# Masking keys from an SBUF copy on VectorE, epsilon inside the normalisation statistics, and a new instruction order, in a four-block attention kernel

## The chip, the cores and the metric

The kernel runs on one core of one Trainium2 chip. The metric is the time of one execution on the device, in microseconds (us). A core has TensorE (PE in the profile, with PEld for its weight loads), VectorE (DVE), ScalarE (ACT), GpSimd (POOL) and SyncE (SP), each with its own queue of instructions that runs in order; engines wait for each other through semaphores. SP, ACT and POOL also issue DMA transfers. SBUF is the working memory, PSUM the eight banks that TensorE writes its results to.

## The reference

The input x is 2048 tokens of 512 numbers in bfloat16. Four blocks follow each other, each with a normalisation in front and a residual behind: linear attention (A), attention in a sliding window of 256 tokens (B), and the same two again with the same weights.

```python
def _layernorm(x, axis=-1, eps=1e-5):
    m = jnp.mean(x, axis=axis, keepdims=True)
    v = jnp.var(x, axis=axis, keepdims=True)
    return (x - m) / jnp.sqrt(v + eps)

# A: 32 heads of 16
phi = lambda t: jnp.where(t > 0, t + 1, jnp.exp(t)) + 1e-6
pq, pk = phi(q), phi(k)
kv = jnp.einsum("bhsd,bhse->bhde", pk, v)
z = jnp.einsum("bhsd->bhd", pk)
o = jnp.einsum("bhqd,bhde->bhqe", pq, kv) / (jnp.einsum("bhqd,bhd->bhq", pq, z)[..., None] + 1e-6)

# B: 32 heads of 16, W = 256
scores = jnp.einsum("bhqd,bhkd->bhqk", q, k) * (Dh ** -0.5)
mask = (idx[:, None] - idx[None, :] >= 0) & (idx[:, None] - idx[None, :] < W)
o = jnp.einsum("bhqk,bhkd->bhqd", _softmax(jnp.where(mask, scores, -1e9)), v)

x = x + _A_ref(_layernorm(x), A_wqkv, A_wo)
x = x + _B_ref(_layernorm(x), B_wqkv, B_wo)
x = x + _A_ref(_layernorm(x), A_wqkv, A_wo)
x = x + _B_ref(_layernorm(x), B_wqkv, B_wo)
```

## The kernel before

The tokens are cut into 16 tiles of 128, which stay in SBUF (`xres`) from start to end. The work has three passes. Pass 1 (operations named `1.`) normalises each tile and sums the keys and values of the first A block. Pass 2 finishes that block tile by tile (`2.`), does the first B block (`2.b.` for queries, keys and values, `2.a.` for the attention) and, as tiles become final, sums the keys and values of the second A block (`2k.`). Pass 3 finishes the second A block (`3.`) and does the second B block (`3.b.`, `3.a.`). Pass 2 can't begin its A outputs before pass 1 has summed all tiles, nor pass 3 before `2k.` has.

**Normalisation** (`ln`, lines 808 to 821). For each of 64 tiles VectorE takes statistics of the 512 numbers (`.st`, line 813), which are two triples, one for every second number; aggregates them into mean and variance (`.ag`, line 814); and adds epsilon to the variance (`.ae`, line 816). GpSimd raises that to the power -1/2 (`.rs`, line 817), and VectorE subtracts and multiplies (`.xn`, line 819). The result is transposed, by a DMA that SP issues (line 827), or for a few tiles (`BYPE`) by TensorE with a copy out of PSUM (lines 834 and 844).

**Keys of a B tile** (`b_qkv`, lines 960 to 983). TensorE computes the projected keys into one PSUM bank (`k0`, `k1`, eight small multiplies each, line 869). The key matrix that the scores use, `kbd`, holds each block of 64 keys twice, once with every second group of 16 rows set to zero and once with the others, so that one multiply of 32 rows serves two heads. Two operations `kb0` and `kb1` write these two forms, both from PSUM, each multiplying by a column of zeros and ones (`mab`), on ScalarE or VectorE as the order says (line 970). Queries and values are copied out of PSUM once each (`qc`, `vc`, line 844), and GpSimd issues four DMAs for each tile that spread the values (`vbd`, line 980).

**Attention of a B tile** (`b_attn`, lines 985 to 1139). TensorE computes scores for the window in five steps into pairs of PSUM banks (lines 1006 and 1055), ScalarE takes exponentials of 128x1024 (lines 1034 and 1076), VectorE masks the ends of the window (lines 1042 and 1094), TensorE multiplies by the values (lines 1112 and 1124), VectorE divides (lines 1134 and 1136), and the output projection and residual follow (lines 857 and 893). The last tile of pass 3 goes through `b_end`, cut finer.

**Order.** Nothing is ordered at run time. `ORDER` (lines 328 to 430) is a list of operation numbers written out in advance: the position in it gives each engine's sequence, an apostrophe takes the second of two possible engines, and what follows a colon names the buffers taken. `schedule` walks through the list, and `emit` sets the waits that the data need. The costs written in the operations (0.595 and so on) take part only in the choice of buffers where the list names none. Operations are numbered as the code creates them, so one that is added or left out shifts all the later numbers. The operations called `jump` stand for a branch in each engine's queue, and where they stand in the list is where the engine branches.

**Loads.** SP issues the tiles of x and most weights (`load`, line 774), and the same queue carries the DMA transposes. In the list before, SP issues x, then the twelve transposes of pass 1's tiles from tile 4 on, then four of the five weights that pass 2 needs, the fifth later.

Of the kernel before, what the change touches and what calls it, by code (L numbers as in the profile page):

```python
# [8 lines left out]
ACT = mybir.ActivationFunctionType  # L9
# [3 lines left out]
P = 128  # L13
D = 512
# [304 lines left out]
def _act_cost(n):  # L319
    return 0.055 + 0.000833 * n  # L320
# [29 lines left out]
933 476:3 477:3 939:1 672:5.1 673 962:6.0.2 961 686:4.0 963 964 700 487:2.3 488 701 674' 934 702:3 687 688 689 489 490 491:0 492:0 940:5 941 942 943:0  # L350
1019:0.6.2 1020 1021 501 944 690:3.2 691 987 478:2 954:0.4.0 955 956 692' 953 1022 479 678 1416:3.1 1417 716 993:0.6.4 1418' 911:5 912 965 994 995 480 913
1419 966:0.3.5 703:3 967 711:2.2.0 502:6.1 945:1 660 661 957 503 504 505 493:5 494 495 968 969 712 713 997:0.3.1 998 999 506:2 970:5 975:2 971 1054:0.6.0 717
718 719 734 735 972 976 977 1055 1056 752 753 989:0.3.0 679 990 973:2 974:3 978:3 979 1000 704:5.1 988 705 706' 707' 736 708:2.3 737 996 709 710' 714 991 992
1028:0.6.3 1029 1030 1420 1421 720:1 507:3 508:4 1422 693:5.1.1 694 695' 1001:0.2.2 1002 1003 509 510 946:7 947 948 1032:0.5.5 1033 1005:4 1006 1004 1423:2
980:2 1034 738:0 511:7.12.1 1010:3 1433 1434 1435 1007 721:2 1008:0 1009:0 1089:0.5.1 981:2 982 1090 1091 1058 1436 512 1424:0 696 697 515 513 1437:3 770
1411:4.1.0 1412 983 1447 1448 1449 1450 1024:0.5.0 1025 1026 1011 1012 1013:1 1014 1031 726:7.0 727 728' 1413 1414 1415 1063:0.2.4 722:6.2 723 1451:1 1027
# [15 lines left out]
1509:1 1510:9 818' 1234:0.6.0 1235 1538 1539:2 1220:2 1705:3.17.3 1241 1236 1237 1706 1221 1222 1223:0 1224 1709 786 1540:8 2716 1273:0.4.4 1274 1461:7.6 1462
# [995 lines left out]
```

## Time and profile before

| | |
|---|---|
| median of 3 runs | 419.46 us (419.31 to 419.74) |
| span of the profiled execution, first to last instruction | 417.1 us |
| granted TensorE clock | 1.000 |
| exponentials on ScalarE, 128x1024 from PSUM | 240 + 56, mean 1.10 us each |
| DMA, mean over the span | 71 GB/s |

Of the profiled execution only the span is recorded, not its time with what lies around it; the median is 2.4 us above the span. In the views that follow an engine's busy time counts the stretch in which at least one of its instructions was open, so two neighbours that overlap are not counted twice; the mean of one instruction is its whole duration, overlap included. A chain of waits is followed back from the last instruction, at each step to whatever released it. "Idle before" is the time for which an engine stood without work in front of an instruction, with the engine that ended it.

### The profile page before, as it was taken

To read this page: it belongs to the slowest core of one execution; us is meant where nothing else is said; L and a number is where in the kernel's file an instruction comes from. 1 tells how busy PE (TensorE), PEld (TensorE's weight loads), DVE (VectorE), ACT (ScalarE), POOL (GpSimd) and SP (SyncE) were. 2 spreads that over 40 slices of the span, in tenths; PEclk is the share of its full clock that TensorE was granted. 3 is DMA by queue.
4 is the path that set the end of the run, shared out by engine and by line. 5 is a ranking of instruction groups with operands and counts; after the bars stand their busy time and mean duration, and the time that the engine had idled before them with its cause. 6 is when DMAs were issued, how large, how long until landed. Compare 5 with 4: busy or idle time off the path is not lost.

```text
span 417.1 us, 18964 instructions
## 1 busy us (share of the span) xinstructions
PE 401.3 (96%) x8402; PEld 283.5 (68%) x8402; DVE 379.2 (91%) x998; ACT 383.3 (92%) x499; POOL 106.7 (26%) x202
## 2 busy tenths in 40 slices
PE   8999999999999999999999999889999999999997
PEld 3654776765767686776686677567676676677775
DVE  6999899999999999999898899999999998979784
ACT  4977979999999999999999677899999999999996
POOL 2331024521343022124150101161333113404100
DMA  8436435343243222324112201331445253243142
GB/s 273 135 63 166 113 53 123 75 55 61 54 77 51 40 48 48 41 53 85 35 40 57 43 2 39 65 81 32 81 66 82 50 72 63 55 85 54 38 93 79
DMA packets 76808, 29.48 MB, mean 71 GB/s; under 512 B 66352, under 2 KB 74672, under 8 KB 76720
## 3 DMA queue, kind: packets, MB, share of 16 engines
q1 hardware_dynamic: 71424, 22.63, 27.0%
q0 software_dynamic: 4096, 4.46, 5.8%
q8 instruction: 68, 1.11, 1.2%
q10 hardware_dynamic: 1200, 1.11, 0.8%
q14 instruction: 20, 0.16, 0.1%
HBM read 6.29 MB, written 2.10 MB: 20 GB/s over the span
## 4 chain that ended last, share of the span: by engine, by line
ACT 47%; PE 41%; DVE 10%; issue 1%; DVEq 0%
ACT pF L1076 33%; PE ps L857 17%; ACT pH L1034 9%; PE ps L869 8%; PE ps L1055 4%; PE ps L1124 4%; PE ps L1112 2%; PE ps L915 2%; ACT kbd L970 2%; DVE o L953 1%; DVE xres L892 1%; DVE stats L813 1%; ACT E L878 1%; PE ps L1253 1%; ACT vt L844 1%
## 5 line engine op out<-in xcount | busy, mean ns | idle before, releaser
L1076 ACT ACTIVATE pF<-ps 128x1024 bf16<-128x1024 f32 x240 | 231.0, 1095 | 2.7 <-PE ps L1055 2.0
L817 POOL TENSOR_TENSOR rstd<-mv,const 128x1 f32<-128x1 f32 x64 | 39.7, 622 | 208.9 <-DVE mv L816 200.1
L980 POOL DMA_DIRECT2D vbd<-vt x128 | 67.0, 532 | 81.1 <-DVE vt L844 61.6
L1034 ACT ACTIVATE pH<-ps 128x1024 bf16<-128x1024 f32 (+1 forms) x64 | 60.5, 1032 | 3.1 <-PE ps L1006 3.0
L1124 PE MATMUL ps<-vbd,pF 128*128 128x34 bf16 x1856 | 59.6, 178 | 0.0
L1124 PEld LDWEIGHTS ps<-vbd,pF 128*128 128x128 bf16 x1856 | 52.9, 96 | 3.3 <-issue 0.2
L1055 PE MATMUL ps<-qT,kbd 32*128 32x128 bf16 x1920 | 49.0, 216 | 4.4 <-ACT pF L1076 1.2
L1094 DVE TENSOR_TENSOR pF<-pF,const 128x512 bf16<-128x512 bf16 (+2 forms) x116 | 46.7, 414 | 4.8 <-ACT pF L1076 4.6
L878 ACT ACTIVATE E<-ps 128x512 bf16<-128x512 f32 x64 | 39.5, 635 | 8.4 <-PE ps L857 4.3
L813 DVE BATCH_NORM_STATS2 stats<-xres 128x6 f32<-128x512 bf16 x64 | 43.8, 687 | 1.9 <-DMA xres<-in_A_x_dram 1.1
L1055 PEld LDWEIGHTS ps<-qT,kbd 32*128 32x128 bf16 x1920 | 28.7, 92 | 22.8 <-ACT pF L1076 9.4
L1042 DVE TENSOR_TENSOR pH<-pH,const 128x1024 bf16<-128x1024 bf16 (+1 forms) x64 | 40.8, 650 | 0.0
L857 PE MATMUL ps<-w_Bv,xT 128*128 128x512 bf16 (+2 forms) x152 | 35.7, 346 | 0.3 <-ACT vt L844 0.2
L869 PE MATMUL ps<-xT,w_Bk 128*128 128x128 bf16 x512 | 35.3, 219 | 0.3
L869 PE MATMUL ps<-xT,w_Bq 128*128 128x128 bf16 x512 | 35.2, 219 | 0.1
L857 PE MATMUL ps<-w_Ao,oT 128*128 128x512 bf16 (+2 forms) x144 | 34.5, 356 | 0.7 <-ACT pF L1076 0.6
L1112 PEld LDWEIGHTS ps<-vbd,pH 128*128 128x128 bf16 x928 | 28.6, 96 | 8.8 <-issue 1.8
L857 PE MATMUL ps<-w_Ak,xTa 128*128 128x512 bf16 (+1 forms) x134 | 33.6, 369 | 0.6 <-ACT xTa L844 0.5
L869 PE MATMUL ps<-xTa,w_Aq 128*128 128x128 bf16 x512 | 33.9, 219 | 0.2
L1112 PE MATMUL ps<-vbd,pH 128*128 128x34 bf16 x928 | 32.9, 178 | 1.1 <-ACT pF L1076 0.3
L857 PE MATMUL ps<-w_Bo,oT 128*128 128x512 bf16 (+2 forms) x140 | 33.0, 355 | 0.7 <-ACT pF L1076 0.6
L857 PE MATMUL ps<-w_Av,xTa 128*128 128x512 bf16 (+2 forms) x133 | 33.6, 371 | 0.0
(95 smaller groups left out, 622.4 us busy)
## 6 DMA issues: line engine op xcount, KB each, us to landing
vbd<-vt POOLq DMA_DIRECT2D x128, 34.0 KB, 2.1
xres<-in_A_x_dram SPq DMA_DIRECT2D x16, 128.0 KB, 4.9
out_dram<-xres SPq DMA_DIRECT2D x15, 128.0 KB, 1.9
oT<-o SPq DMA_TRANSPOSE x60, 2.6
w_Ak<-in_A_wqkv_dram ACTq DMA_DIRECT2D x1, 512.0 KB, 4.8
w_Av<-in_A_wqkv_dram ACTq DMA_DIRECT2D x1, 512.0 KB, 5.8
w_Aq<-in_A_wqkv_dram SPq DMA_DIRECT2D x1, 512.0 KB, 6.2
w_Ao<-in_A_wo_dram SPq DMA_DIRECT2D x1, 512.0 KB, 4.0
```

The lines of the kernel that those rows point to most:

```text
L813: s.op(n + ".st", {"DVE": 0.595}, lambda e, en: e.bn_stats(a_st, x.h[:]), reads=[x], writes=[st])
L857: i = e.matmul(g.h[:, a:b], xT.h[:, kt, :], w.h[:, kt, a:b], start=(kt == 0), stop=(kt == 3), skip_group_check=True)
L869: i = e.matmul(g.h[:, f * P:(f + 1) * P], w.h[:, kt, f * P:(f + 1) * P], xT.h[:, kt, :], start=(f == 0 and kt == 0), stop=(kt == 3), skip_ ...
L878: s.op(n + ".e", {"ACT": _act_cost(512)}, lambda e, en: e.activation(E.h[:], g.h, ACT.Exp, bias=0.0), reads=[g], writes=[E])
L980: return [e.dma_start(vbd.h[64 * a:64 * a + 64, j, a], vt.h[64 * j:64 * j + 64, a]) for j in range(2)]
L1034: return e.activation(d, c, ACT.Exp, bias=0.0, scale=DH ** -0.5)
L1042: return e.tensor_tensor(v, v, tr, ALU.mult)
L1055: i = e.matmul(ss[r // 2].h[:, r % 2, k * P:k * P + P], kbds[fj[m] // 2].h[32 * r:32 * r + 32, f, fj[m] % 2, :], qT.h[32 * r:32 * r + 32, ...
L1076: s.op("e%d%d" % (u, g), {"ACT": _act_cost(1024)}, lambda e, en, S=ss[g], pb=pb, g=g: e.activation(pb.h[:, 2 * g:2 * g + 2, :], S.h, ACT.E ...
L1094: return e.tensor_tensor(v, v, tr, ALU.mult)
L1112: i = e.matmul(U.h[:, c:c + 34], pH.h[:, 4 * r + f, 64 * a:64 * a + P], vbds[j // 2].h[:, j % 2, :, 4 * f + r, :], start=first[0], stop=Tr ...
L1124: i = e.matmul(U.h[:, c:c + 34], pFs[at[f, m][0]].h[:, r, at[f, m][1] * P:at[f, m][1] * P + P], vbds[fj[m] // 2].h[:, fj[m] % 2, :, 4 * f ...
```

## The change

Four things change.

1. The B block's keys are copied once from PSUM to SBUF (`kc`, in a new ring `kt` of three buffers, on ScalarE or VectorE), and `kb0` and `kb1` then read that copy, on VectorE alone. One tile, tile 0 of pass 3 (`KNEAR`), keeps the old form.
2. The statistics of a tile get nine columns in place of six. The third triple is set once at the start: count 0, mean 0, sum of squares epsilon times 512. The aggregation runs over three triples, and the addition of epsilon (`.ae`) is gone.
3. The order is laid anew from the first to the last operation; the list has 2731 entries in place of 2762 (64 `.ae` fewer, 31 `kc` and 2 memsets more).
4. The scaled identity that the last tile uses (`zb`) is made to wait for the warm-up multiplies that read the same memory. Some costs are written differently.

```diff
 ORDER = """
...
 """
+KNEAR = {("3.b.", 0)}
...
+            self.stats = self.tiles("stats", 1, [P, T, 9], F32)[0]
             self.consts()
...
-            self.stats = self.tiles("stats", 1, [P, T, 6], F32)[0]
...
+            self.r_kt = self.ring("kt", 3, [P, D])
...
+        self.eps = _Buf(None, self.stats)
+        for lo, hi, c in ((6, 8, 0.0), (8, 9, LN_EPS * D)):
+            s.op("consteps", {"POOL": 0.1}, lambda e, en, lo=lo, hi=hi, c=c: e.memset(self.stats[:, :, lo:hi], c), part=[self.eps])
...
-        s.op(n + ".st", {"DVE": 0.595}, lambda e, en: e.bn_stats(a_st, x.h[:]), reads=[x], writes=[st])
-        s.op(n + ".ag", {"DVE": 0.08}, lambda e, en: e.bn_aggr(a_mv, a_st), reads=[st], writes=[mv])
+        st0 = self.stats[:, t, 0:6]
+        s.op(n + ".st", {"DVE": 0.595}, lambda e, en: e.bn_stats(st0, x.h[:]), reads=[x], writes=[st])
+        s.op(n + ".ag", {"DVE": 0.08}, lambda e, en: e.bn_aggr(a_mv, a_st), reads=[st, self.eps], writes=[mv])
         v = self.mv[:, t, 1:2]
-        s.op(n + ".ae", {"DVE": 0.06}, lambda e, en: e.tensor_scalar(v, v, LN_EPS, None, op0=ALU.add), writes=[mv])
...
+        near = (s.at[0], t) in KNEAR
+        kt = None if near else self.r_kt.buf()
+        if kt is not None:
+            self.copy("kc", kt, gk, lambda: (kt.h[:], gk.h), [kt])
         for a in range(2):
             def kb(e, en, a=a):
                 o = kbd.h[:, :, :, a * 64:a * 64 + 64].rearrange("p f j c -> p (f j) c")
-                g, m = gk.h.rearrange("p (b c) -> p b c", c=64), self.mab.h[:, a:a + 1]
+                g, m = (gk.h if near else kt.h[:]).rearrange("p (b c) -> p b c", c=64), self.mab.h[:, a:a + 1]
                 return e.activation(o, g, ACT.Copy, scale=m) if en == "ACT" else e.tensor_scalar(o, g, m, None, op0=ALU.mult)
 
-            s.op("kb%d" % a, {"ACT": _act_cost(512), "DVE": _dve_cost(512)}, kb, reads=[gk, self.mab], part=[kbd])
+            s.op("kb%d" % a, {"ACT": 0.57, "DVE": 0.659} if near else {"DVE": 0.26}, kb, reads=[gk if near else kt, self.mab], part=[kbd])
...
-        s.op("zb", {"DVE": 0.2}, lambda e, en: e.tensor_scalar(big.h, self.ident.h[:], LIFT / ONE, None, op0=ALU.mult), reads=[self.ident, self.zero], writes=[big])
+        zb = s.op("zb", {"DVE": 0.2}, lambda e, en: e.tensor_scalar(big.h, self.ident.h[:], LIFT / ONE, None, op0=ALU.mult), reads=[self.ident, self.zero], writes=[big])
+        for d in s.ops:
+            if d.name in ("warm", "warm2"):
+                zb.deps[d] = False
```

In the new order SP's queue starts with x as before, then one transpose (tile 4 of pass 1), all five weights of pass 2, and then the other transposes. VectorE's branch stands between the first key mask of tile 15 of pass 3 and the reciprocals of its tile 12 (before: ahead of the last tile's reciprocals), GpSimd's in pass 1, ScalarE's about where it stood. The number of changes between scores and other work on TensorE is 304, against 302.

More of the change, by code (lines that the diff above doesn't have):

```diff
@@ L352 @@
[L352 to L355, printed above, removed]
@@ new lines @@
+977 1015 741:1 494:7 495 1417 691':1 692 987:0.5.2 1016 1418 988 989 498 978 724:2 742:0 693 496 1407:0 1419 1420:3 1408:0 1009 1421:2 991:3 990 756 697:4.1.4
+992 993 1018:0.6.5 698 499 996:5 997 998 1019 501 994:2 995:0 1020 699' 500 999:0 1075:0.2.1 1017 967:4 968 1076 1077 757 758 1000 502 700 969 701 1430
+715:7.2.1 1010:0.5.0 1011 1012 716 1431 717' 712:4.0 718 713 1021 719 1049:0.2.4 707:7.2 1396:6.6.3 1397 714' 1013 1050 1051 1022:0.4.1 1008 708 1044 1052
+709':2 1432 1433:2 1023 1398 1399 1409:3.0.1 1024 1400 710 1427:2.2 1410 1428 1026:7 1053:0.4.2 1422:6.4.0 1423 1411 1429' 1025 711 1412 1027 1031:2 1028 1413
@@ new lines @@
+1454 1161 1135:2 1217 1150:0.4.3 1151 1152 518:6.1 519 771' 1473 784:2.0 785 786 1139:3 1140 520 787:3.1.3 788 1189:0.4.4 1190 521 522:1 1157 779:7.0 523:0
+1455:6.1 1456 530 1218 1191 789' 1474:2 1162:0.2.5 780 1486 1487:1 1192 1153 524:5 781':0 542:4.15.2 1457' 1163 1164 543 525 1165 546 782 783 1166:7
+1193:0.2.0 1167 1461:0 1171:6 526 1219 1168 1169:2 544 1170:3 792 1194 1195 1141:1 1475:3 790 1250:0.4.0 1172 1173 1251 1252 772 1142:7 1185:0.2.3 1186 1187
+1462:9 1143 532 793 1174:0 1175 794 545 1481:6.0 1482 1224:0.4.1 547 1144 1476:7.3.3 1477 1483' 1188 795:3 1225 1226 533:2.3 534 1660:6.16.0 1661 773 1478
@@ new lines @@
+1276:4 1277 1274:2 1539 1753 1275:0 1289 1290:0.2.3 1291 1292 826 827 1509:5.6 833:7.3 1510 834 1528:2 1665 1323 1511' 1529:13 1293 1278 835:0 1279:0 1280
+1301 1281:3 1302:0.2.4 1303 838:6.3 839 1306:7 1329:0.4.2 840' 1307 1494:6.2 1540 1495 1304 1330 1331 1324 1755 1308 1309:3 1305 1496' 1333:0.2.5 1468:5.3
+1282:4 1310:1 1334 1335 1283 1325:0.6.3 1469 1630:3.2.2 1631 1284 836 837 1326 1327 1517:4.4.1 1553 1554 1470' 1541:0 1328 1311:2 1555 1337:0.6.1 841:5.0.5
+842 1542:14 1518 1332 1634 843' 1312 1313 1336 1632 1338 1339 1519 1355:0.6.0 1356 1497:5.3 1357 1340 1314:1 1315 1520 1521 1498 1341:2 1342 1343 1344:2 1359
@@ new lines @@
+2284:0.2.1 1958:7.0.5 2285 1953 1944 2286 2194:1 1959 2252:5.0.2 2253 2254 1960' 2247 1955:4.1 1983 1771:2.1 1772 1773 1956 1957 2256:7 2257 1967:3 2276:5.0.0
+2277 1774 2278 2258 1999 1775:0 1954 2230:2 1761:3 2287 1984:0 1762:4 1763 2280:2.5.5 2281 1776:3 2282 2000 2259:0 2260:2 2163:7 1764 2255 2164 2195:4 2165
+2307:0.2.0 2196 1985:4 2261:5 2262 2308 2309 2320:0.6.3 2263 2283 2274 2197 2017 1968:4.4 1969 2264:2 2279 2265 2275 2321 2322 1970':0 1971 2288:0.2.4
+1976:5.2.0 1977 1786:6.3 1787 1828 2292:4 2293 1800 2018 2289 2290 2312:0.2.2 1978 1788 2294 2313 2314 1789 1972 1973:5.2 1790:3 2316:6.0.0 1961 1962 1974
@@ new lines @@
+2295:1 2291 2311 1801:2.0 1802 2296:1 2166 2315 1975' 2266:0 1994:4.1.2 2317 2318 1995 1803 2267:7 2343:5.0.1 2268 1996 2344 2345 1777:4 1778 2310 1804 1979
+2001 2002:3 2319 1805:0 2269 2356:2.5.5 2357 2297:7 2298 2299 2358 1815 1779 2347 2019 2348:0.2.1 2020:1 2300:2 2349 2350 2301 1986:4.5 1987 2328:5 2323
+2324:0.6.4 1997 1988':1 1989 2329 2325 2326 1991:4.3 1830 1845 2035 2359 2330 2331:3 2198 2003:2 1806:1 2332:2 2036 2352:0.2.2 1791:0 2270 2037 1980 1992 1990
+1993' 2353 2354 2351 2038:2 2327 2004:7.0 2005 2006:2 1792:6 1793 2379:0.2.2 2380 2381 1807:7 1808 1794 2355 2053 2346 2231:6 2392:0.4.0 2232 1809 2233 2393
@@ new lines @@
+2394 2054 2055 2333:3 2334 2335 2007 2008 2336:1 2360:0.6.3 2361 2362 1831:4.0 1832 2021:0 2027:2.0 2028 2337 1833 1834 1835:0 1816:0.2 1817 2395 2029 2364:3
+2302:3 2384:4.6.4 1818 1819 2365 2385 2039:1 1820:3 1821:0 2386 2009:2.1 2010 2363 2388:0.4.1 2389 2071 2011' 2366 1998 1846:6.3 1847 2012:2.0.3 1836:1 2367:1
+2368:1 2390 2013 2014 2387 1848 2072 2073 2015 2016 1849 1850:3 2369:3 2428:0.4.2 2074:0 2383 2391 2370 1822:2 2371 2372:0 2373 2382 1851:2 2429 2430 2075:3
+2415:0.6.0 1823 1824 2022:5.1 2023 2416 2024':0 2396:0.3.5 2418 1837:2 1838 1839 2417 2400:5 2397 2398 2399 2056:3 2025 2234 2338:0 2374:1 2420:0.6.3 2421
@@ new lines @@
+2422 2026 2401 2030:4.2.1 2402 2107 2403:2 2424:0.2.4 2404:0 2031 2108 2425 2426 2045:7.2 2046 2032' 2047' 2451:0.5.1 2452 1852:4 1853 2453 2089 2431 2090
+2091 2405:7 2464:0.2.1 2465 2466 1854 2406 2040:6.2 2407 2419 2432:0.4.0 2423 2427 2408:1 2409 2433 2041 2436:3 2437 2438 2057:4 2042':1 2456:0.6.5 2434 2125
+2033 2126 2439:3 2092:1 2440:3 2435 2410:2 2457 2063:2.3 2127 2034 2064 2066:5.1.4 2460:0.3.3 2458 2461 2067 2065' 2441:2 2442 2454 2043 2044 2500:0.6.4 2068'
+2455 2443 2069 2048:5.0.5 2049 2462 2501 2502 2487:0.3.2 2109 2463 2444:0 2445 2084:2.2.0 2488 2058:7.3 2085 2050' 2459 2489 2490 2086' 2492:0.5.2 2059
@@ L430 @@
+2105 2106 2141 2142 2582 2587 2605 2606 2644:0.6.1 2135:5.3 2583:3 2584:3 2588:0 2589 2136 2645 2646 2599 2603 2607 2631:0.2.0 2555:4 2556 2616:7 2632 2137'
[6 rows of a table added]
 """
@@ L812, in ln @@
         a_st, a_mv, a_rs = self.stats[:, t, :], self.mv[:, t, :], self.rstd[:, t:t + 1]
-        s.op(n + ".st", {"DVE": 0.595}, lambda e, en: e.bn_stats(a_st, x.h[:]), reads=[x], writes=[st])
-        s.op(n + ".ag", {"DVE": 0.08}, lambda e, en: e.bn_aggr(a_mv, a_st), reads=[st], writes=[mv])
+        st0 = self.stats[:, t, 0:6]
+        s.op(n + ".st", {"DVE": 0.595}, lambda e, en: e.bn_stats(st0, x.h[:]), reads=[x], writes=[st])
+        s.op(n + ".ag", {"DVE": 0.08}, lambda e, en: e.bn_aggr(a_mv, a_st), reads=[st, self.eps], writes=[mv])
         v = self.mv[:, t, 1:2]
-        s.op(n + ".ae", {"DVE": 0.06}, lambda e, en: e.tensor_scalar(v, v, LN_EPS, None, op0=ALU.add), writes=[mv])
-        s.op(n + ".rs", {"POOL": 0.53}, lambda e, en: e.tensor_tensor(a_rs, v, self.half.h[:], ALU.pow), reads=[mv, self.half], writes=[rs])
+        s.op(n + ".rs", {"POOL": 0.53}, lambda e, en: e.tensor_tensor(a_rs, v, self.half.h[:], ALU.pow),
+             reads=[mv, self.half], writes=[rs])
         xn = self.r_xn.buf()
@@ L839, in transp, with copy @@
         return o
-    def copy(self, n, o, g, aps):
+    def copy(self, n, o, g, aps, new=()):
         def cp(e, en):
@@ L844, in cp @@
             return e.activation(a, b, ACT.Copy) if en == "ACT" else e.tensor_copy(a, b)
-        self.s.op(n, {"ACT": _act_cost(512), "DVE": _dve_cost(512)}, cp, reads=[g], writes=[o])
+        self.s.op(n, {"ACT": _act_cost(512), "DVE": _dve_cost(512)}, cp, reads=[g], writes=[o], new=new)
     def proj_tok(self, n, xT, w, *dst):
@@ L951, in a_out @@
             dn.h[:].rearrange("p (g h) -> p g h", g=2).unsqueeze(3), uv()[:, :, :, 16:17], 1e-6, None, op0=ALU.add), reads=[us], writes=[dn])
-        s.op("dr", {"DVE": 0.17}, lambda e, en: e.reciprocal(dn.h[:], dn.h[:]), writes=[dn], tail=0.11)
+        s.op("dr", {"DVE": 0.275}, lambda e, en: e.reciprocal(dn.h[:], dn.h[:]), writes=[dn])
         s.op("dm", {"DVE": 0.6}, lambda e, en: e.tensor_tensor(
```

80 lines of the change are left out of this document (31 added, 49 removed), and 89 rows, old and new, of the table ORDER.

## The prediction

> **What bounds the kernel now.** I read the page first, for shares and the chain of waits.
>
> ```profile
> span 417.1 us, 18964 instructions
> PE 401.3 (96%) x8402; PEld 283.5 (68%) x8402; DVE 379.2 (91%) x998; ACT 383.3 (92%) x499; POOL 106.7 (26%) x202
> ...
> ACT 47%; PE 41%; DVE 10%; issue 1%; DVEq 0%
> ```
>
> Three engines are above 90% and the chain changes hands between them, so an average tells little. I therefore cut the span where the work changes: at ScalarE's first full-width exponential of tile 2 in pass 2 (65.9), at its last exponential of that pass (233.6), and at the same two places of pass 3 (282.9, 411.6). The windows give, in order, PE, PEld, DVE and ACT busy:
>
> ```profile
> 0.00:65.90 65.90, 63.14 (x611) 38.82 (x612) 59.60 (x196) 50.20 (x88) 15.45 (x34) 1.00 0.50 131
> 65.90:233.60 167.70, 163.82 (x3695) 116.53 (x3696) 157.53 (x398) 165.58 (x203) 46.88 (x86) 1.00 0.32 58
> 233.60:282.90 49.30, 46.73 (x762) 34.24 (x759) 46.57 (x127) 38.64 (x62) 10.37 (x19) 1.00 0.23 46
> 282.90:411.60 128.70, 124.27 (x3301) 91.84 (x3299) 112.72 (x272) 127.54 (x144) 34.03 (x63) 1.00 0.36 65
> 411.60:417.10 5.50, 3.37 (x48) 2.05 (x43) 2.73 (x9) 1.37 (x5) 0.00 (x0) 1.00 0.29 95
> ```
>
> I call these stages 1 to 5. Stage 1 is TensorE's (2.8 us idle). Stages 2 and 4 are ScalarE's (2.1 and 1.2 us idle), with TensorE close behind (3.9 and 4.4). Stage 3, the crossing between the attention passes, is shared by TensorE and VectorE (2.6 and 2.7 us idle), with 10.7 us of ScalarE free. The granted clock is 1.00 throughout.
>
> **The edits and their prices.** Numbering the operations of both orders as the code creates them, I counted each kind by engine and stage. Keys before: 40 masked reads of PSUM on VectorE and 24 on ScalarE. After: one plain copy for 31 of 32 tiles (21 VectorE, 10 ScalarE), 62 masks on VectorE from SBUF, and tile 0 of pass 3 as before, on ScalarE.
>
> ```profile
> L970 DVE TENSOR_SCALAR kbd<-ps,const 128x512 bf16<-128x512 f32 x40 | 28.2, 742 | 0.5 <-PE ps L869 0.4
> L970 ACT ACTIVATE kbd<-ps,const 128x512 bf16<-128x512 f32 x24 | 15.9, 724 | 1.2 <-PE ps L869 1.2
> ```
>
> Durations of neighbours overlap, so what an instruction costs its engine is the distance from its start to the next start. For VectorE, from the timeline:
>
> ```profile
> 53.22 0.18 DVE L814 BATCH_NORM_AGGREGATE mv<-stats 128x2 f32<-128x6 f32 x1
> 53.43 0.15 DVE L816 TENSOR_SCALAR mv<-mv 128x1 f32<-128x1 f32 x1
> 53.50 0.41 DVE L819 TENSOR_SCALAR xn<-xres,mv,rstd 128x512 bf16<-128x512 bf16 x1
> 53.82 0.69 DVE L892 TENSOR_TENSOR xres<-ps,xres 128x512 bf16<-128x512 f32 x1
> ...
> 55.76 0.28 DVE L879 TENSOR_SCALAR E<-E 128x512 bf16<-128x512 bf16 x1
> 55.95 0.34 DVE L952 RECIPROCAL dn<-dn 128x32 f32<-128x32 f32 x1
> ...
> 63.80 0.74 DVE L970 TENSOR_SCALAR kbd<-ps,const 128x512 bf16<-128x512 f32 x1
> 64.46 0.18 DVE L950 TENSOR_SCALAR dn<-ps 128x32 f32<-128x32 f32 x1
> ...
> 128.01 0.69 DVE L844 CAST vA<-ps 128x512 bf16<-128x512 f32 x1
> 128.61 0.68 DVE L884 SCALAR_TENSOR_TENSOR pk<-ps,E 128x512 bf16<-128x512 f32 x1
> ...
> 257.25 0.18 DVE L814 BATCH_NORM_AGGREGATE mv<-stats 128x2 f32<-128x6 f32 x1
> 257.35 0.66 DVE L892 TENSOR_TENSOR xres<-ps,xres 128x512 bf16<-128x512 f32 x1
> ```
>
> A masked PSUM read costs 0.66, a plain one 0.60. For a mask from SBUF to SBUF there is no row; it lies between the clamp without a per-partition operand (55.76 to 55.95, 0.19) and the normalisation with two of them (53.50 to 53.82, 0.32). The mask has one, so I take 0.26 and keep both ends. VectorE has 98 reads of PSUM for keys, queries and values before (40 and 58) and 77 after: 61.2 becomes 46.2, and 62 x 0.26 = 16.1 comes on top: +1.1 (bounds -3.2 and +4.8).
>
> The epsilon add goes 64 times. It costs 0.07 where something else fills its wait, and with the wait behind the aggregation 0.28 - 0.10 = 0.18 (53.22 to 53.50 against 257.25 to 257.35). At 0.10 this is -6.4 (-4.5 to -11.5). Aggregating nine numbers instead of six costs between nothing and half of its 0.10 more, 3.2 in all; I take nothing, the whole instruction being nearly fixed cost. Two more memsets on GpSimd lie in its idle time (74%).
>
> ScalarE, from the chain of waits:
>
> ```profile
> 97.45 5.50 ACT pF L1076 x6
> ...
> 197.07 0.98 ACT vA L844 x2
> 201.72 1.14 ACT kbd L970 x2
> ```
>
> So 0.92 an exponential, 0.49 a copy, 0.57 a mask. By the new order it has per stage: stage 1 five masks fewer and five copies more (-0.4); stage 2 twelve masks and two exponentials fewer, four feature-map passes fewer, five copies more (-6.8 - 1.8 - 2.0 + 2.4 = -8.2); stage 3 what was moved there (+3.3); stage 4 five masks fewer, three copies more (-1.4).
>
> TensorE's work is the same in sum but moved:
>
> ```profile
> 13.20 0.86 PE ps L857 x4
> 14.06 0.89 PE ps L869 x16
> ...
> 139.94 0.40 PE L1055 MATMUL ps<-qT,kbd 32*128 32x128 bf16 x16
> 140.27 0.57 PE L1124 MATMUL ps<-vbd,pF 128*128 128x34 bf16 x16
> ```
>
> A half projection is 0.43 or 0.445, a block of scores with its turn 0.33. Stage 1 loses one half projection (-0.4); stage 2 eight and a block of scores (-3.9); stage 3 gains twelve, one block and four turns (+5.9); stage 4 -0.4; stage 5 -0.4 to -1. VectorE in the same way, with the prices above: stage 2 -4.8, stage 3 +8.1 (copies, output adds and masks that stood in stages 2 and 4), stage 4 about -6.8.
>
> **A moved queue.** On SP's queue five weight loads of 512 KB now stand in front of the transposed load of tile 5 of pass 1; before, four of them came after all twelve transposes.
>
> ```profile
> 12.29 23.80 SPq L827 DMA_TRANSPOSE xTa<-xn  x12
> 36.14 0.58 SPq L774 DMA_DIRECT2D w_Ao<-in_A_wo_dram  x1
> ...
> 37.87 0.51 SPq L774 DMA_DIRECT2D w_Bv<-in_B_wqkv_dram  x1
> ```
>
> The DMA issues and the timeline of TensorE:
>
> ```profile
> w_Ao<-in_A_wo_dram SPq DMA_DIRECT2D x1, 512.0 KB, 4.0
> ...
> w_Bv<-in_B_wqkv_dram SPq DMA_DIRECT2D x1, 512.0 KB, 6.3
> ```
>
> ```profile
> xTa<-xn SPq DMA_TRANSPOSE x1, 4.1
> ```
>
> ```profile
> 20.06 1.03 PE L857 MATMUL ps<-w_Av,xTa 128*128 128x512 bf16 x4
> ```
>
> The four loads landed in their order, at 36.14 + 4.0 = 40.1 to 37.87 + 6.3 = 44.2, so 1.35 us apart. The first transpose (12.29) landed at 16.4, 4.1 after issue, behind the last loads of x. In the new order the loads go out after that issue, from about 13.8: the first lands at 17.8, the fifth 5.4 later at 23.2, and tile 5's transpose, if it queues behind them, about 1.1 after that, 24.3. TensorE's first use of tile 5 was at 20.06, its 36th operation; it is now the 34th, 0.4 us earlier, 19.6. That is a stall of 4.7 us, with all later projections queued behind it in order, and ScalarE and VectorE soon without input. At the other bound the transpose overtakes and, sent at 16.3, lands 4.1 later: 0.8, nearly nothing. What speaks for the full stall is that loads on this queue landed in order. [...]
>
> ScalarE's preset fills move forward in stage 1, into its 15.7 idle microseconds: nothing. VectorE's branch moves from before the last tile's reciprocals to before those of tile 12, into stage 4; they and tile 13's masks queue behind it, and tile 12's output projection waits for them. ScalarE's branch lies in this gap:
>
> ```profile
> 237.79 0.60 ACT L844 ACTIVATE oT<-ps 128x512 bf16<-128x512 bf16 x1 [2.97 <-PE ps L834]
> ```
>
> So up to 2.97; VectorE's 16.0 idle us of stage 4 and its relief there cover it, and I take nothing. The added waits of the last tile's scaled identity are on work done 400 us earlier.
>
> **The sum.** Stage 1: +4.7, of which I let 1.1 be made up in TensorE's 2.8 idle us, and -0.4: +3.2. Stage 2: between TensorE's -3.9 and ScalarE's -8.2: -6.0. Stage 3: TensorE's +5.9 less its 2.6 of idle time gives +3.3, VectorE's +8.1 whole is the other end; nearer to the low end, as the moved work waits on nothing of the crossing: +4.6. Stage 4: -0.4 to -1.4: -0.9. Stage 5: -0.4. Together +0.5 on the span of 417.1. The runs' median is 419.46, so 2.4 us lie around the span, unchanged: **420.0**.
>
> **Rivals.** (1) *No stall*: the transpose is not held up. Stage 1 is then -0.4, the sum -3.1: 416.4. For it: one TensorE position is all that shows the need; against it: the landings in order. (2) *The crossing decides*: its length is set by the serial run of statistics, projections and scores, so VectorE's +8.1 is added whole while stage 2 gives only TensorE's -3.9. That is 5.6 above the sum: 425.6. It is slower than before from the point where stages 2 and 3 together give less than 1.9 (3.2 - 0.9 - 0.4). For it: VectorE was 94% busy there; against: the moved work is independent. (3) *TensorE has room*: stage 2 gives ScalarE's whole -8.2 and stage 3 only +3.3, 3.5 below the sum: 416.5. [...] (4) *Dear masks*: a mask costs 0.66 as from PSUM. The extra 0.40 is hidden in stages 2 and 4 (24 masks, 9.6 each, against VectorE's 10.2 and 16.0 idle us) but not in 1 and 3 (8 and 6 masks): +5.6, 425.6. [...]
>
> **How the numbers follow.** Chances: the forecast 0.45, no stall 0.25, crossing 0.15, dear masks 0.08, TensorE's room 0.07. Changes under 0.2% (0.84 us) can't be told from none. The forecast's own range is 417.0 to 423.5, which falls about equally to faster (0.13), same (0.16) and slower (0.16); with the rivals that is faster 0.45, same 0.16, slower 0.39. Cases of both signs hold most of the chance; the range runs from below the two fast rivals, 413.0, to just under the two slow ones, 425.0.
>
> **What would show it.** A TensorE gap of 4 to 5 us before the second-half projection of tile 5, near 20 us, with the weights landing until 23 (stall; its absence is rival 1). Masks starting 0.26 apart. ScalarE's last exponential of pass 2 about 3 us earlier than 233.6 in spite of the stall. A crossing of 54 us rather than 57. I am wrong altogether if the crossing keeps its 49 us or if stage 2 doesn't get shorter.

## The result, and the profile after

The changed kernel takes 429.48 us (428.31 to 429.77, 4 runs), the one before 419.6: a ratio of 1.0229 (95% interval 1.0211 to 1.0247). The prediction, 420.0 with a range up to 425.0, was wrong, and none of its rivals reached this time either (the slowest were at 425.6). The profiled execution took 429.26, 1.4 more than its span. From the page of after:

```profile
span 427.9 us, 18833 instructions
...
PE 393.9 (92%) x8309; PEld 287.3 (67%) x8388; DVE 370.7 (87%) x977; ACT 379.1 (89%) x487; POOL 105.9 (25%) x204
...
PEclk9989998998999999999999999999999999999999
...
PE 47%; ACT 23%; DVE 15%; DMA 11%; issue 2%; POOL 0%; SPq 0%; DVEq 0%; POOLq 0%
```

None of the three large engines is busier than before; they wait more. DMA, absent from the chain of before, holds 11% of it. The page now has a line for the granted clock, with three eights; the page of before has no such line, its mean granted clock being 1.000.

The stages must be cut at the same operations as before. Two marks need care. In pass 2 the order of tile 15's exponentials changed: ScalarE's last pair of before now comes second to last, and the stage ends, as in my count of the work, at the end of that pair. From ScalarE's timeline of after:

```profile
236.85 1.94 ACT L1086 ACTIVATE pF<-ps 128x1024 bf16<-128x1024 f32 x2 [0.23 <-PE ps L1065]
238.67 0.60 ACT L884 ACTIVATE E<-ps 128x512 bf16<-128x512 f32 x1
...
240.72 1.94 ACT L1086 ACTIVATE pF<-ps 128x1024 bf16<-128x1024 f32 x2 [0.95 <-PE ps L1065]
```

And tile 2 of pass 3 began at 277.18 in the kernel before, not at the 282.9 that the prediction cut at. The windows of before with that boundary (columns as in the prediction, then GpSimd's busy time, the granted clock, the DMA share and GB/s):

```profile
233.60:277.18 43.58, 41.38 (x657) 30.30 (x653) 41.06 (x115) 33.14 (x57) 7.20 (x13) 1.00 0.20 39
277.18:411.60 134.42, 129.63 (x3405) 95.78 (x3405) 118.23 (x284) 133.04 (x150) 37.20 (x70) 1.00 0.37 66
```

and of after:

```profile
0.00:74.36 74.36, 64.76 (x601) 40.40 (x611) 55.16 (x179) 50.57 (x89) 14.73 (x36) 0.95 0.54 124
74.36:238.70 164.34, 155.53 (x3594) 115.74 (x3629) 152.53 (x382) 158.24 (x191) 46.84 (x85) 0.99 0.32 55
238.70:287.27 48.57, 45.70 (x717) 34.04 (x724) 44.02 (x117) 36.78 (x62) 10.51 (x20) 1.00 0.26 48
287.27:422.60 135.33, 124.66 (x3357) 95.01 (x3381) 116.29 (x293) 132.58 (x148) 33.82 (x64) 1.00 0.36 63
422.60:427.90 5.30, 3.24 (x50) 2.12 (x46) 2.69 (x9) 0.92 (x4) 0.00 (x0) 1.00 0.23 74
```

| stage | before | after | change | forecast |
|---|---|---|---|---|
| 1 | 65.9 | 74.36 | +8.5 | +3.2 |
| 2 | 167.7 | 164.34 | -3.4 | -6.0 |
| 3 (crossing) | 43.58 | 48.57 | +5.0 | +4.6 |
| 4 | 134.42 | 135.33 | +0.9 | -0.9 |
| 5 | 5.5 | 5.30 | -0.2 | -0.4 |
| span | 417.1 | 427.9 | +10.8 | +0.5 |

The stages add up to 10.8, the times differ by 9.9. In every run of the kernel before that has both numbers the time is 1.2 to 1.4 us above the span, so its profiled execution, with a span of 417.1, was probably about 1 us faster than the median.

Half of the miss is stage 1. SP's queue, the landing of tile 5's transpose (issued at 16.94; last figure, us from issue to landing), and TensorE's timeline:

```profile
16.36 0.53 SPq L779 DMA_DIRECT2D w_Bo<-in_B_wo_dram  x1
16.94 10.99 SPq L833 DMA_TRANSPOSE xTa<-xn  x6
```

```profile
xTa<-xn SPq DMA_TRANSPOSE x1, 8.0
```

```profile
20.35 0.59 PE L863 MATMUL ps<-w_Ak,xTa 128*128 128x512 bf16 x2
25.02 2.57 PE L863 MATMUL ps<-w_Av,xTa 128*128 128x512 bf16 x8 [4.07 <-DMA xTa<-xn]
27.38 1.91 PE L863 MATMUL ps<-w_Ak,xTa 128*128 128x512 bf16 x4
```

The transpose landed at 16.94 + 8.0 = 24.9 (forecast 24.3), and the gap is 4.07 (forecast 4.7). But then four wide multiplies take 1.91 us, where the prediction's rows had 0.86. The windows of after around the gap, whose third number from the end is the granted clock, say why:

```profile
24.30:26.30 2.00, 1.28 (x6) 0.52 (x7) 1.91 (x7) 0.00 (x0) 1.51 (x3) 1.00 1.33 189
26.30:29.70 3.40, 3.40 (x10) 1.22 (x9) 0.36 (x2) 0.97 (x2) 0.00 (x0) 0.50 0.34 77
29.70:31.70 2.00, 1.95 (x25) 1.51 (x24) 1.45 (x5) 1.74 (x5) 0.61 (x1) 1.00 0.00 0
```

For 3.4 us TensorE has half its clock: 1.7 us of work lost. It happens twice more, after a gap of 2.18 at the start of pass 2 and one of 1.98 in stage 2:

```profile
66.30 1.07 PE L875 MATMUL ps<-xT,w_Bk 128*128 128x128 bf16 x16 [2.18 <-DMA xT<-xn]
67.21 1.85 PE L875 MATMUL ps<-xT,w_Bq 128*128 128x128 bf16 x16
...
105.25 0.63 PE L863 MATMUL ps<-w_Ao,oT 128*128 128x512 bf16 x1 [1.98 <-DMA oT<-o]
```

```profile
67.30:70.70 3.40, 3.40 (x48) 3.12 (x46) 2.02 (x7) 2.17 (x4) 0.56 (x1) 0.50 0.34 62
104.80:108.20 3.40, 2.61 (x52) 1.83 (x55) 1.07 (x4) 1.45 (x3) 0.00 (x0) 0.50 0.00 0
```

All of these gaps end on a transpose. TensorE's longest waits of after (total, times, longest); the same view of before lists none on a transpose:

```profile
PE ps L863 <- DMA xTa<-xn: 5.1, 2, 4.1
PE ps L863 <- DMA oT<-o: 4.9, 6, 2.0
...
PE ps L875 <- DMA xT<-xn: 3.2, 3, 2.2
```

### The profile page after: what moved, and what is told of

Same layout as the page of the kernel before. It is cut to its first block, busy times and chain, and to the rows that moved or that the text cites. A ratio compares the mean times of both kernels' runs of the same rounds, so it can differ in the third digit from the quotient of the medians.

```text
span 427.9 us, 18833 instructions
## 1 busy us (share of the span) xinstructions
PE 393.9 (92%) x8309; PEld 287.3 (67%) x8388; DVE 370.7 (87%) x977; ACT 379.1 (89%) x487; POOL 105.9 (25%) x204
## 4 chain that ended last, share of the span: by engine, by line
PE 47%; ACT 23%; DVE 15%; DMA 11%; issue 2%; POOL 0%; SPq 0%; DVEq 0%; POOLq 0%
PE ps L863 19%; ACT pF L1086 17%; PE ps L875 10%; PE ps L1134 5%; PE ps L1065 5%; DMA oT<-o 5%; ACT pH L1044 5%; DMA xT<-xn 3%; PE ps L1122 3%; DVE stats L819 2%; DVE o L959 2%; DMA xTa<-xn 2%; PE ps L1016 2%; PE ps L921 2%; DMA xres<-in_A_x_dram 1%
## 5 line engine op out<-in xcount | busy, mean ns | idle before, releaser
L822 POOL TENSOR_TENSOR rstd<-mv,const 128x1 f32<-128x1 f32 x64 | 38.5, 607 | 192.0 <-DVE mv L820 182.7
L1134 PE MATMUL ps<-vbd,pF 128*128 128x34 bf16 x1856 | 60.7, 178 | 0.0
L1134 PEld LDWEIGHTS ps<-vbd,pF 128*128 128x128 bf16 x1856 | 54.4, 96 | 7.0 <-issue 0.6
L875 PE MATMUL ps<-xT,w_Bk 128*128 128x128 bf16 x512 | 36.9, 222 | 3.5 <-DMA xT<-xn 2.4
L875 PE MATMUL ps<-xT,w_Bq 128*128 128x128 bf16 x512 | 36.6, 222 | 1.4 <-DMA xT<-xn 0.8
L863 PE MATMUL ps<-w_Ao,oT 128*128 128x512 bf16 (+2 forms) x122 | 30.5, 357 | 7.0 <-DMA oT<-o 4.2
L875 PEld LDWEIGHTS ps<-xT,w_Bk 128*128 128x128 bf16 x512 | 30.1, 99 | 8.8 <-DMA xT<-xn 2.8
L863 PE MATMUL ps<-w_Ak,xTa 128*128 128x512 bf16 (+2 forms) x123 | 33.2, 382 | 1.3 <-issue 0.7
L875 PEld LDWEIGHTS ps<-xT,w_Bq 128*128 128x128 bf16 x512 | 30.2, 99 | 5.0 <-DMA xT<-xn 1.3
```

The costliest lines, as they stand in the source:

```text
L863: i = e.matmul(g.h[:, a:b], xT.h[:, kt, :], w.h[:, kt, a:b], start=(kt == 0), stop=(kt == 3), skip_group_check=True)
L875: i = e.matmul(g.h[:, f * P:(f + 1) * P], w.h[:, kt, f * P:(f + 1) * P], xT.h[:, kt, :], start=(f == 0 and kt == 0), stop=(kt == 3), skip_ ...
L1134: i = e.matmul(U.h[:, c:c + 34], pFs[at[f, m][0]].h[:, r, at[f, m][1] * P:at[f, m][1] * P + P], vbds[fj[m] // 2].h[:, fj[m] % 2, :, 4 * f ...
```

## The experiments

Times are medians; each ratio is against the kernel before in runs of the same chip. "Old order" is that of the kernel before, "new order" that of the changed one. Edits of the order are shown by the names of operations.

| kernel | us | ratio (95%) |
|---|---|---|
| a_loads_back | 423.41 | 1.0096 (1.0068 to 1.0123) |
| b_loads_fwd | 426.43 | 1.0169 (1.0150 to 1.0188) |
| b_loads_two | 419.36 | 1.0008 (0.9996 to 1.0020) |
| b_loads_three | 421.98 | 1.0055 (1.0036 to 1.0075) |
| a_loads_act | 426.45 | 1.0177 (1.0128 to 1.0226) |
| a_keep_pe | 431.99 | 1.0279 (1.0243 to 1.0315) |
| old_both | 422.71 | 1.0092 (1.0067 to 1.0116) |
| old_eps | 418.12 | 0.9977 (0.9962 to 0.9991) |
| old_keys | 424.92 | 1.0140 (1.0107 to 1.0174) |
| old_near | 418.96 | 1.0001 (0.9991 to 1.0011) |
| new_oldkeys | 427.97 | 1.0206 (1.0171 to 1.0241) |
| new_add | 423.70 | 1.0121 (1.0067 to 1.0176) |

**The loads, undone and done alone.**

```diff
 1.4:ln.xT
-load_Ao load_Bk load_Bq load_Bv load_Bo
 ... 1.15:ln.xT
+load_Ao load_Bk load_Bq load_Bv load_Bo
```

> The changed kernel with one thing undone: SP issues the five weight loads of pass 2 behind the twelve transposes of pass 1 again; every other place in the order is the new one. Theory L (the moved loads are the loss): the first full-width exponential of tile 2 comes at 65 to 67 instead of 74.4, the granted clock stays at 1.00 to 60, and the time falls by 7 to 9 us, to 420.5 to 422.5. Rival N (the new order is slower by itself, the stall only covers what would be waited for anyway): 426 to 430. Whatever is left above 419.6 less the 6.9 that the forecast had for the remaining stages is then the relief of pass 2 that did not come.

The reverse edit on the kernel before:

> The kernel before with that one thing done: the five weight loads issued right behind the first transpose. Theory L with the clock: a gap of 4 to 5 us on TensorE near 20, a granted clock under 0.9 behind it, and 426.5 to 428.5, that is 7 to 9 us slower. Rival S (only the stall counts, the clock's fall is made up): 423 to 424.5. Rival N: within 2 us of 419.6.

Undone: 423.41, 6.1 less than 429.48, with the mark of tile 2 at 66.80. Done alone: 7.0 more. Theory L holds on both sides in kind; undone it is 6, where it had 7 to 9. The stages of a_loads_back, without the fifth:

```profile
0.00:66.80 66.80, 60.80 (x601) 38.64 (x611) 54.67 (x179) 50.12 (x89) 15.15 (x36) 1.00 0.54 136
66.80:234.00 167.20, 156.58 (x3593) 115.32 (x3629) 152.30 (x382) 158.72 (x190) 46.73 (x85) 0.99 0.33 55
234.00:283.34 49.34, 45.91 (x717) 33.94 (x724) 44.11 (x117) 37.05 (x62) 10.51 (x20) 1.00 0.29 46
283.34:416.47 133.13, 124.59 (x3356) 94.79 (x3380) 116.08 (x293) 132.12 (x148) 33.89 (x64) 1.00 0.34 64
```

Against before: +0.9, -0.5, +5.8, -1.3. In stage 2 ScalarE is busy for 158.7 us instead of 165.6 and the stage is just 0.5 shorter: what ScalarE was spared became idle time. But something new stands in this stage: TensorE waits 4.2 us for transposes, where the kernel before lists no such wait (total, times, longest):

```profile
PE ps L875 <- DMA xT<-xn: 1.6, 2, 1.3
...
PE ps L863 <- DMA xTa<-xn: 1.2, 1, 1.2
...
PE ps L863 <- DMA xT<-xn: 0.8, 1, 0.8
...
PE ps L863 <- DMA oT<-o: 0.6, 2, 0.3
```

A half-clock stretch (granted 0.50) from 175.5 to 178.9 costs up to 1.7 more. Four us above the kernel before remain that the loads don't explain.

**How many loads.**

```diff
 1.4:ln.xT
+load_Ao load_Bk
 1.5:ln.xT ... 1.15:ln.xT
-load_Ao load_Bk
 load_Bq load_Bv
```

> The kernel before with two of the five loads (w_Ao and w_Bk) behind the first transpose and the rest where they were. All five gave a gap of 6.27 us on TensorE and 426.4. Theory P (the gap is the bytes ahead: some 1.1 to 1.35 us for each 512 KB, and three loads less take 3.3 to 4 us off it): a gap of 2.2 to 3 us, 421 to 423. Rival C (the fall of the clock is most of the price, and comes with any gap of 2 us): 423 to 425. Rival Z (two loads land in time): 419 to 420.

With load_Bq moved too:

> The kernel before with three of the five loads (w_Ao, w_Bk, w_Bq) behind the first transpose. Two gave a gap of 1.05 us on TensorE, no fall of the clock and 419.4; five gave 6.27 us, two windows of 3.41 us at half clock and 426.4. Theory G (by bytes: (6.27 - 1.05) / 3 = 1.74 us of gap for each further load, of which pass 1 makes up about one microsecond in all): a gap of 2.5 to 3.1 us; without a fall of the clock 421 to 421.8, with one (half of 3.41 us more) 422.5 to 423.5. Rival H (three loads still land in time): 419 to 420. Rival J (the whole price comes with the third load): 425 to 427.

TensorE at tile 5, with two, three and five loads ahead (b_loads_two, b_loads_three, b_loads_fwd):

```profile
21.63 0.81 PE L858 MATMUL ps<-w_Av,xTa 128*128 128x512 bf16 x3 [1.05 <-DMA xTa<-xn]
```

```profile
23.33 0.81 PE L858 MATMUL ps<-w_Av,xTa 128*128 128x512 bf16 x3 [2.88 <-DMA xTa<-xn]
```

```profile
26.79 1.49 PE L858 MATMUL ps<-w_Av,xTa 128*128 128x512 bf16 x3 [6.27 <-DMA xTa<-xn]
```

Two loads cost nothing that can be told (rival Z, not my 2.2 to 3 us of gap), three a gap of 2.88 and 2.7 us in all, five a gap of 6.27, where I had expected 4 to 5, with 6.8 us at half clock, and 7.0 in all. From two on each further load adds 1.7 to 1.8 us of gap (theory G). With three loads the clock fell in some of the runs: two at a mean clock of 0.996 took 423.09 and 422.60, four at 1.000 took 420.71 to 422.54, mean 421.45. The difference, 1.4, is about the 1.7 of one half-clock window.

**Another queue.** The same place in the list, but ScalarE issues:

```diff
-            wload(n, "SP", c, c + D, 14.2 + 1.8 * i)
+            wload(n, "ACT", c, c + D, 14.2 + 1.8 * i)
```

> The changed kernel with the five weight loads at their new place in the order but issued by ScalarE on its own queue, SP's queue holding only x, Aq and the transposes. Theory Q (the transposes wait because they stand behind the loads in one queue): tile 5's transpose lands by 20.5, the gap is under 1 us, and the time is that with the loads behind, 422 to 424.5. Rival B (the 2.5 MB fill the DMA engines and the transposes share them, whatever the queue): the gap stays at 3 to 5 us and the time at 427 to 430.

Tile 5's transpose now stands behind no load on SP. Its issue, and its landing among the DMA issues from 13.2 to 16 us:

```profile
14.41 2.08 SPq L833 DMA_TRANSPOSE xTa<-xn  x1
```

```profile
xTa<-xn SPq DMA_TRANSPOSE x1, 8.6
```

The same view of the kernel before:

```profile
xTa<-xn SPq DMA_TRANSPOSE x3, 2.6
```

Issued ahead of three of the five loads, in another queue, it still took 8.6 us and landed at 23.0. So theory Q falls for the transposes. Queue, packets, MB and share of the 16 DMA engines' time from 14.4 to 23.0, the loads being in q10 and the transposes in q1:

```profile
q10 hardware_dynamic: 1940, 1.93, 92.3%
q1 hardware_dynamic: 590, 0.14, 8.4%
```

In the kernel before, from 14 to 20:

```profile
q1 hardware_dynamic: 1855, 0.44, 36.8%
```

Together the two queues fill the engines (100.7%), which fits rival B's reading that loads and transposes share them, whatever the queue. The time, 426.45, lies between the two forecasts, and isn't a clean measure of either, as ScalarE was held for 2.92 us by its own issues and TensorE for 2.68 us behind it. So late, TensorE found tile 5 landed, and then waited 2.50 us for a later transpose.

**Filling the gap.**

```diff
 1.3:k1
+busy   (17 multiplies 128x512)
 1.5:v0
```

> The changed kernel with 17 idle-time multiplies of 128x512 into a free bank, whose result nobody reads, put in front of the second-half projection of tile 5 that waits for the late transpose: TensorE has 3.65 us of work in the 4.07 us gap. Theory C (the gap lets the clock fall, and the fall costs its own time): the clock stays at 1.00 from 25 to 31, the multiplies there take 5.0 us instead of 7.0, and the time falls by 1.5 to 2.5 us, to 427 to 428. Rival R (the slow stretch is hidden or its time is lost elsewhere): 429 to 430. Rival W (the added work comes late and lengthens the gap): above 430.

TensorE in a_keep_pe:

```profile
22.40 3.83 PE L1345 MATMUL ps<-w_Av,const 128*128 128x512 bf16 x16
27.92 2.00 PE L863 MATMUL ps<-w_Av,xTa 128*128 128x512 bf16 x8 [1.68 <-DMA xTa<-xn]
29.76 1.03 PE L863 MATMUL ps<-w_Ak,xTa 128*128 128x512 bf16 x4
```

Here theory C's stretch came out: the clock stayed at 1.00, and the work that took from 25.02 to 32.06 in after takes from 27.92 to 33.29, 5.37 instead of 7.04 us. The whole did not gain: 431.99, in rival W's range, two runs at a mean clock of 1.000 taking 429.24 and 432.04. The profiled run is no clean measure: it had a half-clock stretch from 8.3 on, was 1.6 us late before the gap, and its tile 5 came 2.9 us later than in after (27.92 for 25.02). The fall's price in its stretch is shown; that removing it saves time in this kernel is not, and why not stays open.

**The edits without the new order.** old_both keeps the old order:

```diff
 old order
-ln.ae (64 times)
-kb0 (first place, its engine)   kb1
+kc  (first place, its engine)   kb0 kb1 (DVE)
```

> Both edits (keys copied once and masked on VectorE, epsilon as a third triple) in the order of the kernel before: each copy stands where the first of the two masks stood and on its engine, both masks on VectorE where the second stood, or ten places later where that was ScalarE's. Theory G (the edits gain by themselves, the new order wastes it): 413 to 418. Rival E (the masks on VectorE cost what ScalarE is spared): 419 to 421. Rival V (VectorE becomes the bound): above 422.

> The order of the kernel before with the epsilon edit alone (statistics of nine columns, no addition; keys as before). Both edits in that order took 422.7, 3.3 more than before. Theory K (the key edit costs it: the chain from the projected keys to the scores is an instruction longer, and where TensorE bounds a stage nothing is gained): 417 to 420 here. Rival E (the third triple costs: an aggregation of nine numbers or the memsets at the start): 421.5 to 424.

> The order of the kernel before with the key edit alone (one copy, two masks on VectorE from SBUF; epsilon added as before). Theory K: 422 to 425, the loss in the first tiles of pass 2 (about 2 us between the end of pass 1 and tile 2's first full-width exponential) and in the first tiles of pass 3. Rival E: 419 to 421.

The wait of `zb` (the fourth change) is in these kernels too. Both edits lose 3.3, epsilon alone gains 0.9 (0.23% by the ratio), and the key edit alone loses 5.9, at the upper end of theory K's range. The two alone add up to 5.0; the 1.7 between this and 3.3 is the size of one half-clock stretch, which all four runs of old_keys have by their mean clocks and one of the four of old_both. The loss has a place: from the sums of pass 1 to tile 2's first full-width exponential old_keys takes 26.7 us where the kernel before takes 22.4; over the rest of pass 2 it loses 1.3 more, and afterwards nothing, where theory K had a loss in pass 3 too. Tile 0 in old_keys, ScalarE and then VectorE:

```profile
56.82 0.60 ACT L850 ACTIVATE kt<-ps 128x512 bf16<-128x512 f32 x1 [0.48 <-PE ps L875]
...
61.82 1.08 ACT L1044 ACTIVATE pH<-ps 128x512 bf16<-128x512 f32 x2 [3.51 <-PE ps L1016]
```

```profile
60.28 0.42 DVE L888 TENSOR_TENSOR pq<-pq,E 128x512 bf16<-128x512 bf16 x1
60.62 0.61 DVE L980 TENSOR_SCALAR kbd<-kt,const 128x512 bf16<-128x512 bf16 x2
```

The keys are out of PSUM at 57.4, but the masks stand behind other work on VectorE until 60.6, and ScalarE is idle for 3.51 us for want of scores. A fall of the clock follows (61.1 to 64.5, 0.50), and is part of the loss. In all TensorE waits 4.3 us for masks on VectorE in old_keys, and 3.9 in old_both, where the kernel before lists no such wait. The kernel before, on ScalarE:

```profile
56.61 1.26 ACT L970 ACTIVATE kbd<-ps,const 128x512 bf16<-128x512 f32 x2 [0.49 <-PE ps L869]
...
58.86 1.09 ACT L1034 ACTIVATE pH<-ps 128x512 bf16<-128x512 f32 x2 [0.50 <-PE ps L1006]
```

ScalarE wrote both masks itself and had its scores 3 us sooner. Part of the loss is where I put the masks. So old_near gives the first three tiles their old form back:

```diff
-KNEAR = {("3.b.", 0)}
+KNEAR = {("3.b.", 0), ("2.b.", 0), ("2.b.", 1), ("2.b.", 2)}
```

> Both edits in the order of the kernel before (422.7 there), but tiles 0, 1 and 2 of pass 2 keep their two masks from PSUM, at their old places and engines, as tile 0 of pass 3 does. Theory F (the key edit costs its 2.3 to 4.6 us in the first tiles, where the scores wait for copy and masks one after the other on two queues): tile 2's first full-width exponential at 65 to 66, and 418 to 419.5 in all. Rival V (the masks' load on VectorE costs everywhere): 421.5 to 423.

418.96, with tile 2's mark at 65.16: theory F. The other 28 tiles' masks on VectorE, at the places I gave them, cost about 1 us against old_eps by the two ratios, and gain nothing.

**The new order with one edit undone** (loads behind, as in a_loads_back):

```diff
 new order
-kc            kb0 kb1 (DVE)
+kb0 kb1 (at kc's place, on its engine)
```

> The new order with the weight loads behind pass 1's transposes and the keys masked from PSUM twice, both at the place and on the engine of the copy (22 masks on ScalarE, 42 on VectorE); epsilon as a third triple. With the new keys this order took 423.4. Theory K says that it falls here too, to 419 to 422; rival O (the order is laid out for the cheap copies, and with the bank held longer and ScalarE loaded more it loses): 424 to 428.

With the addition back behind each aggregation:

> The new order with the weight loads behind pass 1's transposes, the new keys, and epsilon added to the variance again, 64 instructions on VectorE each right behind its aggregation. Theory: the triple is worth 0.07 to 0.18 us for a tile where VectorE decides and nothing elsewhere, so 0 to 4 us more than 423.4: 423.5 to 427. Rival E: 420 to 422.5.

The old keys cost the new order 4.6 us: rival O, not K. That the order is laid out for the cheap copies is rival O's reason and not shown by itself. The addition costs 0.3 there by the medians and 1.0 by the ratios, less than the intervals tell. The fastest kernel of all is old_eps, 0.23% ahead of before, and 2.5% ahead of the change by the two ratios.

## Why the prediction was wrong

Two terms of the sum failed. For stage 1 (+3.2, measured +8.5) the prediction had one gap at full clock, of which a part was to be made up; there were two gaps, each with a stretch at half clock, and nearly nothing was made up. For stage 2 (-6.0, measured -3.4) it took the work that leaves the engines as time, with nothing for new waits; TensorE waited there for transposes, and the clock fell once more.

*The stall on SP's queue.* The size was right (24.9 for 24.3, 4.07 for 4.7). Two steps around it were wrong. "Of which I let 1.1 be made up in TensorE's 2.8 idle us": nearly nothing was made up. And "the granted clock is 1.00 throughout" was carried over to a kernel with gaps. The sums of pass 1 on VectorE, in after and in a_loads_back:

```profile
50.45 0.79 DVE L1232 TENSOR_TENSOR kvz<-ps,const 128x272 bf16<-128x272 f32 x2 [0.90 <-PE ps L921]
```

```profile
44.82 0.79 DVE L1232 TENSOR_TENSOR kvz<-ps,const 128x272 bf16<-128x272 f32 x2 [0.90 <-PE ps L921]
```

With the loads back they come 5.6 us earlier: about the 4.07 of the gap and 1.7 of the clock. The second fall, at 67.3, is absent there too, and from these sums to tile 2's mark it takes 22.0 us instead of 23.9. This term, +3.2 for +8.5, is the largest error of the sum. The reason given, loads and transpose in one queue, was not the whole one: with separate queues the transpose takes as long from its issue (8.6 us for 8.0).

*Stage 2, -6.0 between TensorE's -3.9 and ScalarE's -8.2.* It gave -3.4, a little under the low bound, and -0.5 in a_loads_back. ScalarE did lose its work (158.7 us for 165.6 in a_loads_back), and TensorE's waits for transposes (2.9 us on `oT` in after, 4.2 in all in a_loads_back) and a fall of the clock (1.7 in each) came in its place. The sum had no term for either. What the stage would give without them no run shows, so how much ScalarE's relief is worth beyond TensorE's share stays open. Rival 3, TensorE has room, did not come: the stage gave 3.4, not ScalarE's whole 8.2. Whether because TensorE has no room or because of these waits, the traces don't separate.

*The crossing, +4.6.* Near in size, +5.0, but in part by luck. TensorE's busy time grew by 4.3 us, not 5.9, and VectorE's by 3.0, not 8.1; the 2.6 us of TensorE's idle time that were to be filled were not (2.2 before, 2.9 after). I had also cut its end at a wrong mark, so that its 54 us are 48 from the mark used here. "ScalarE's last exponential of pass 2 about 3 us earlier than 233.6" was wrong in any reading: the pair that ended at 233.6 ends at 238.7, the last one at 242.7.

*The masks, 0.26.* Right. From VectorE's timeline of after:

```profile
178.33 0.61 DVE L980 TENSOR_SCALAR kbd<-kt,const 128x512 bf16<-128x512 bf16 x2
178.86 0.41 DVE L825 TENSOR_SCALAR xn<-xres,mv,rstd 128x512 bf16<-128x512 bf16 x1
```

Two masks in 0.53 us. Rival 4, dear masks, falls. What the prediction lacked is the edit's other cost: it prices engine time, and not the longer chain from projection to scores at the start of pass 2, where the scores are awaited. In the new order that stretch is no longer than before (22.0 us in a_loads_back, 22.4 before), and TensorE waits for no mask there, so this cost is not seen in the changed kernel.

*The aggregation of nine, nothing; the addition, 6.4 in sum of engine time.* The first is right within 9 ns (below). The second was worth 0.9 us in the old order.

*Stages 4 and 5.* -0.9 and -0.4 against +0.9 and -0.2; in a_loads_back, with the same order there, stage 4 is -1.3. The difference between these two I can't explain from one trace of each.

*The 2.4 us around the span.* Too much by about 1: the runs of both kernels have 1.2 to 1.4, and the profiled execution of before was probably a fast one. It put the forecast about 1 us too high, so it did not cause the miss.

*What stays open.* a_loads_back is 4.0 us above before. By its stages that is the crossing's +5.8, the work moved there having bought only 0.5 in stage 2, where the waits for transposes and the fall of the clock stand. TensorE waits in the new order for transposes that the old one had in time, 8.0 us in all in a_loads_back. It is the order that brings these waits, and not the edits: they come to 0.4 us in old_both, and to 4.7 in new_oldkeys. Which step of the order does it wasn't tried. Part of the four us is the clock: of a_loads_back's seven runs the one at a mean clock of 1.000 took 421.07, the six at 0.995 or 0.996 took 422.24 to 425.06.

## What to carry to other kernels

Work taken off an engine is not yet time off the stage: here ScalarE lost 6.9 us in stage 2 and the stage got 0.5 to 3.4 shorter, because other waits came in, while what was moved to the crossing made that longer by 5.0 to 5.8. So list for each stage what else will be awaited there, transposes above all, before its relief goes into the sum. A transfer brought forward must be weighed against every short transfer that is awaited while it runs: here a transpose took 8.0 us to land with the loads in its own queue and 8.6 with them in another, where the kernel before has 2.6. When a copy is put between a producer and its users, look at the first tiles, where the chain is awaited, and leave those as they were.

## What the runs showed of the hardware

*TensorE's clock dropped after short gaps.* Gaps of 4.07, 2.18 and 1.98 us (after) were each followed or overlapped by 3.4 us at a granted 0.50, one of 6.27 (b_loads_fwd) by 6.8 us. Behind gaps of 2.68 and 2.50 in a_loads_act, at a mean clock of 0.992, eight wide multiplies took 3.02 us and four took 1.71; in a_keep_pe four took 1.03 at 1.00. With the gap of 2.88 (b_loads_three) the clock fell only in two runs of six. Gaps of 1.8 (a_loads_back), 1.68 (a_keep_pe) and 1.05 (b_loads_two, none of ten runs) brought no fall. In a_loads_back one fell at 175.5 with no gap over 1.06 us just ahead of it. So in these runs a gap of two or three microseconds cost up to 1.7 more, in some executions and not in others; where the bound lies, and what is counted, these runs don't settle. TensorE was not idle throughout ahead of a fall: in the 3.4 us ahead of the one at 104.8 (after) it was busy for 1.87.

*Transposes by DMA were slower with loads on another queue:* tile 5's took 8.6 us to land in a_loads_act, with the loads on ScalarE's queue, where the kernel before has 2.6.

*Aggregating nine numbers cost hardly more than six:* 185 ns in the mean against 176. From the groups of instructions of after, and of before:

```profile
L820 DVE BATCH_NORM_AGGREGATE mv<-stats 128x2 f32<-128x9 f32 x64 | 11.6, 185 | 0.5
```

```profile
L814 DVE BATCH_NORM_AGGREGATE mv<-stats 128x2 f32<-128x6 f32 x64 | 11.1, 176 | 1.2
```
